# Retention followed by mixture of depths on one core: loads four ahead, a later fetch, q in 2 KB packets, a cap that also sums

## The chip, the core and the metric

The kernel runs on one core of a Trainium2 chip. The core has five engines with an instruction queue each: TensorE (PE in the profile; PEld are its weight loads), VectorE (DVE), ScalarE (ACT), GpSimd (POOL) and SyncE (SP), and 16 DMA engines that they share. The metric is the device time of one execution in microseconds; the median of three runs of the kernel before is 142.53 us (141.37 to 142.64).

## The reference

Two layers in a row. The first is a linear attention with decay, per batch (4), head (8) and token (768), with heads of 64. The second lets the 128 best-scored tokens of each batch through an expert with one hidden layer and leaves the others as they are.

```python
# q, k, v: [4, 8, 768, 64] float32
for t in range(S):
    state = gamma[None, :, None, None] * state + np.einsum('bhd,bhe->bhde', k[:, :, t], v[:, :, t])
    y[:, :, t] = scale * np.einsum('bhd,bhde->bhe', q[:, :, t], state)
...
x = y.transpose(0, 2, 1, 3).reshape(B, S, H * D)        # [4, 768, 512]
scores = np.einsum('bsd,d->bs', x, w_gate)
out = x.copy()
for b in range(B):
    top_idx = np.argpartition(-scores[b], capacity)[:capacity]      # capacity 128
    xe = x[b, top_idx]
    h = np.maximum(xe @ w1, 0.0)                                    # w1 [512, 1024]
    ye = h @ w2                                                     # w2 [1024, 512]
    g = 1.0 / (1.0 + np.exp(-scores[b, top_idx]))
    out[b, top_idx] = x[b, top_idx] + g[:, None] * ye
```

## The kernel before

The 768 tokens of a batch are three blocks of 256 (two chunks of 128 each); the four batches make 12 blocks, m = 0 to 11. The text calls the body of the main loop for block m "turn m".

**Loads and stores, on SP's queue.** `load(m)` (L54 to L63) brings q, k and v of a block, 512 KB each, into SBUF in float32. A partition holds two neighbouring tokens of all eight heads, so a contiguous piece is 512 bytes (two tokens of 64 floats). There are five buffers for each, and turn m begins with `load(m + 5)`. `put(m, xo)` (L246) stores the block's 256 output rows in two DMAs of 256 KB, one for the even and one for the odd tokens. SP works through its queue in order: block m's store stands behind load m + 5.

**Casts, on GpSimd.** `cast(m)` (L147) makes bfloat16 copies: q times a table of decays `gq`, k as it is, v times a table `gv`. Turn m casts block m + 2. GpSimd's queue also has the four DMAs of the expert's weights (w1s, w2s, in turns 1 to 4), the fetch of a batch's chosen rows, a product for the gate and the scatter of the result (`route_put`).

**A turn, on TensorE, VectorE and ScalarE.** In this order: the q transposes of block m + 1 (`transposes`, L159: eight on TensorE into PSUM, then one copy by ScalarE, L170); the second half of the block's own scores (`scores`, L173: 16 matmuls, then VectorE's multiply with the causal mask, L185); the state of the first chunk (`update`, L212); the k transposes of block m + 1; the outputs (`inside`, `across`, L191 to L210); `finish` (L232: ScalarE copies the output to SBUF, VectorE forms the token scores, `junk`, L242); the second chunk's state; `put`; the first half of the scores of block m + 1. Even and odd tokens of a chunk are kept as two halves, so the tokens of a row of scores stand as (even, odd), and the mask, the token numbers and the store are laid out for it.

**Routing and expert.** A batch's routing is written into slots of later turns by hand (`at(turn, place, ...)`, L404 to L419, run by `slot_work`). Place -1 is at the start of the turn before the casts, 0 to 4 lie between the steps above. In the turn after each block, `route_spread` (L259) turns a block's scores into a row and `route_beats` (L273) counts with VectorE which tokens beat which. After the batch's last block `route_beats` also caps the counts at 128 (`wonb`, L290, 128x5 elements), `route_ranks` (L295) adds up ranks on TensorE and `route_index` (L312) turns them into the 128 row numbers. One turn after that, `route_fetch` (L323) gathers the 128 rows from the output in HBM. It reads what `put` wrote, so it waits until the stores of the batch have landed; it is an instruction of GpSimd's queue and stands ahead of that turn's cast. Two turns later come `route_gate` and `route_turn` (the rows are transposed), then the expert: `ffn_up` twice, `ffn_down`, and in the next turn `ffn_add` (L386, VectorE), and then `route_put`, the scatter. The slots of turns 12 and later are worked off one after the other behind the loop.

The slots of a batch whose last block is m (L408 to L419) are, with turns counted from m: ranks and index at 1, fetch at 2, gate and turn at 4, expert at 5, add at 6, scatter at 7. The last blocks of the batches are 2, 5, 8 and 11.

Of the kernel before, what the change touches and what calls it, by code (L numbers as in the profile page):

```python
# [18 lines left out]
def kernel(ctx: ExitStack, tc: tile.TileContext, q, k, v, w_gate, w1, w2, capacity, out):  # L19
    nc = tc.nc  # L20
    B, H, S, D = q.shape
    C = 128
    NC = S // C
    T = 2 * C
    NM = S // T
    Dm = H * D
    F = w1.shape[1]
    cap = int(capacity)
# [22 lines left out]
    ctx.enter_context(tc.manual_schedule())  # L51


    raw = {}  # L54

    def load(m):
        b, r = divmod(m, NM)
        for nm, src in (("q", q), ("k", k), ("v", v)):
            t = loads.tile([128, H, 2, D], FT, name=nm + "f", tag=nm + "f")
            ap = src[b, :, r * T:(r + 1) * T, :]  # L60
            ap = bass.AP(tensor=ap.tensor, offset=ap.offset, ap=[[2 * D, 128], ap.ap[0], [1, 2 * D]])
            nc.sync.dma_start(t.rearrange("p h j d -> p h (j d)"), ap)
            raw[nm, m] = t  # L63

    load(0)
# [3 lines left out]

    pos_i = consts.tile([128, NM, 2], I32)
    nc.gpsimd.iota(pos_i, pattern=[[T, NM], [1, 2]], base=-MID, channel_multiplier=2)
    pos = consts.tile([128, 2 * NM], FT)
    nc.vector.tensor_copy(pos, pos_i.rearrange("p a b -> p (a b)"))
    lnsc = consts.tile([128, 1], FT)
    nc.vector.memset(lnsc, lnscale)
    gq = consts.tile([128, 2 * NM, H], FT)
    gv = consts.tile([128, 2 * NM, H], FT)
    for h in range(H):  # L80
        nc.scalar.activation(gq[:, :, h], pos, AF.Exp, bias=lnsc[:, 0:1], scale=lng[h])
    for h in range(H):
        nc.scalar.activation(gv[:, :, h], pos, AF.Exp, scale=-lng[h])
    ident = consts.tile([128, 128], BF)
# [2 lines left out]
    make_identity(nc, identf)  # L87

    causal = consts.tile([128, 2, 2, 64], BF)
    nc.gpsimd.memset(causal, 1.0)
    for u in range(2):
        rows = slice(u * 64, u * 64 + 64)
        nc.gpsimd.affine_select(out=causal[rows], in_=causal[rows], pattern=[[-1, 2], [1, 2], [2, 64]],
                                compare_op=OP.is_ge, fill=0.0, base=0, channel_multiplier=-2)

    ones = consts.tile([128, 128], BF)
# [5 lines left out]

    load(2)
    load(3)
    load(4)
    before = consts.tile([128, C], FT)
    tokrow = consts.tile([128, S], FT)
    slotcol = consts.tile([128, 1], FT)  # L110
# [1 line left out]
    def route_tables():  # L112
        nc.gpsimd.memset(before, TINY)
        nc.gpsimd.affine_select(out=before, in_=before, pattern=[[1, C]], compare_op=OP.is_gt,
                                fill=-TINY, base=0, channel_multiplier=-1)
        slot_i = consts.tile([128, 1], I32)
        nc.gpsimd.iota(slot_i, pattern=[[0, 1]], base=0, channel_multiplier=1)
        tok_i = loads.tile([128, S], I32, name="toki", tag="toki", bufs=1)
        nc.gpsimd.iota(tok_i.rearrange("p (c j t) -> p c j t", j=2, t=64), pattern=[[C, NC], [1, 2], [2, 64]],
                       base=0, channel_multiplier=0)  # L120
        nc.gpsimd.tensor_copy(slotcol, slot_i)
        nc.gpsimd.tensor_copy(tokrow, tok_i)
# [24 lines left out]
    def cast(m):  # L147
        r = m % NM
        kb = nats.tile([128, 2, H, D], BF, name="kb", tag="kb")
        vb = nats.tile([128, 2, H, D], BF, name="vb", tag="vb")  # L150
        qb = nats.tile([128, 2, H, D], BF, name="qb", tag="qb")
        nc.gpsimd.tensor_mul(qb, raw["q", m].rearrange("p h j d -> p j h d"),  # L152
                             gq[:, 2 * r:2 * r + 2, :, None].to_broadcast([128, 2, H, D]))
        nc.gpsimd.tensor_copy(kb, raw["k", m].rearrange("p h j d -> p j h d"))  # L154
        nc.gpsimd.tensor_mul(vb, raw["v", m].rearrange("p h j d -> p j h d"),  # L155
                             gv[:, 2 * r:2 * r + 2, :, None].to_broadcast([128, 2, H, D]))
        nat[m] = (kb, vb, qb)

    def transposes(m, nm):  # L159
        src = nat[m][2 if nm == "q" else 0]  # L160
        if nm == "q":
            pt = psT.tile([128, HP, 2, 2, 64], BF, name="pt", tag="pt")
        else:
            pt = psT.tile([128, 2, HP, 128], BF, name="pt", tag="pt")
        for j in range(2):
            for dd in range(HP):
                o = pt[:, dd, :, j, :] if nm == "q" else pt[:, j, dd, :]
                nc.tensor.transpose(o, src[:, j, 2 * dd:2 * dd + 2, :], ident)  # L168
        t = work.tile(list(pt.shape), BF, name=nm + "T", tag=nm + "T")
        nc.scalar.activation(t, pt, AF.Copy)  # L170
        tr[nm, m] = t

    def scores(m, part):  # L173
        qT, kT = tr["q", m], tr["k", m]
        pa = psA.tile([128, 2, 2, 2, C], FT, name="pa", tag="pa")
        for d in range(2):
            dd = 2 * part + d
            for j in range(2):
                for u in range(2):
                    for half in range(2):  # L180
                        r = slice(half * 64, half * 64 + 64)
                        nc.tensor.matmul(pa[u * 64:u * 64 + 64, half, d, j, :], kT[r, j, dd, u * 64:u * 64 + 64],  # L182
                                         qT[r, dd, u].rearrange("p j t -> p (j t)"), start=True, stop=True)
        am = work.tile([128, 2, 2, 2, C], BF, name="am", tag=f"am{part}")
        nc.vector.tensor_mul(am.rearrange("p a b c d -> p (a b) (c d)"), pa.rearrange("p a b c d -> p (a b) (c d)"),  # L185
                             causal.rearrange("p a b c -> p (a b c)")[:, None, :].to_broadcast([128, 4, 2 * C]))
        att[m, part] = am


# [13 lines left out]
    def across(m, u, py):  # L203
        i = 2 * m + u
        if i % NC == 0:
            return
        qT = tr["q", m]
        for dd in range(HP):
            nc.tensor.matmul(py[u][:, 2 * dd:2 * dd + 2, :], qT[:, dd, u].rearrange("p j t -> p (j t)"),  # L209
                             S_sb[i % 2][:, dd, :], start=False, stop=True, skip_group_check=True)  # L210

    def update(m, u):  # L212
# [32 lines left out]

    def put(m, xo):  # L246
        b, r = divmod(m, NM)
        for j in range(2):
            ap = out[b, r * T:(r + 1) * T, :]
            ap = bass.AP(tensor=ap.tensor, offset=ap.offset + j * Dm, ap=[[2 * Dm, 64], [C * Dm, 2], [1, Dm]])  # L250
            nc.sync.dma_start(ap, xo[j * 64:(j + 1) * 64])


    flat = out.rearrange("b s d -> (b s) d")
# [18 lines left out]
    def route_beats(b, r):  # L273
        st = batch[b]
        row, g, pr, won = st["row"], st["beats"], st["pr"], st["won"]
        if r:
            for u in range(2):
                c = 2 * r + u
                nc.vector.tensor_scalar(g[:, c, :r * T], row[:, :r * T], st["sc"][:, c:c + 1], float(c * C),
                                        OP.is_lt, OP.subtract, accum_out=won[:, c:c + 1])  # L280
        for u in range(2):
            c = 2 * r + u
            nc.vector.scalar_tensor_tensor(g[:, c, c * C:(c + 1) * C], pr[:, u, :], st["sc"][:, c:c + 1], before,
                                           OP.subtract, OP.is_lt)
        c = 2 * r + 1
        nc.vector.tensor_scalar(g[:, c, r * T:c * C], pr[:, 0, :], st["sc"][:, c:c + 1],
                                won[:, c:c + 1] if r else float(C), OP.is_lt, OP.subtract, accum_out=won[:, c:c + 1])
        if r == NM - 1:
            wonb = perb.tile([128, NC], BF, name="wonb", tag="wonb")
            nc.vector.tensor_scalar_min(wonb[:, 1:], won[:, 1:], float(cap))  # L290
            st["wonb"] = wonb


# [107 lines left out]
    def at(t, place, f, *args):  # L401
        slots.setdefault((t, place), []).append((f, args))

    for m in range(NBLK):  # L404
        b, r = divmod(m, NM)
        at(m + 1, 0, route_spread, b, r)
        at(m + 1, 1, route_beats, b, r)
        if r == NM - 1:  # L408
            at(m + 1, 3, route_ranks, b)
            at(m + 1, 4, route_index, b)  # L410
            at(m + 2, -1, route_fetch, b)
            at(m + 4, -1, route_gate, b)
            at(m + 4, 2, route_turn, b)
            at(m + 4, 4, route_sigmoid, b)
            at(m + 5, 0, ffn_up, b, 0)
            at(m + 5, 2, ffn_up, b, 1)
            at(m + 5, 3, ffn_down, b)
            at(m + 6, 1, ffn_add, b)
            at(m + 7, -1, route_put, b)  # L419

    def slot_work(t, place):
        for f, args in slots.pop((t, place), ()):
# [73 lines left out]
```

## Time and profile before

| | us |
|---|---|
| median of three runs | 142.53 |
| the profiled execution | 140.93 |
| its span, first to last instruction | 139.2 |
| TensorE busy (59% of the span) | 82.3 |
| VectorE busy (56%) | 77.7 |
| GpSimd busy (55%) | 76.7 |
| ScalarE busy (49%) | 67.6 |

No engine is busy for more than 59% of the span, and TensorE's mean granted clock is 0.843. DMA: SP's queue moved 25.43 MB in 41,040 packets, GpSimd's 4.20 MB in 2,240. From issue to landing a load takes 7.3 to 7.7 us, a store 5.3, a gather 4.6 (medians).

A line of a group or of a timeline names the line of the program, the engine, the operation and its tiles as output<-input. In the timeline the first number is the start in us and the second the duration; a bracket gives the idle time before it and what ended that. In the list of waits the three numbers are the us in total, the number of times and the longest. A row of windows has the stretch, its length, the busy time of PE, PEld, DVE, ACT and POOL with the number of instructions, the granted clock, the share of the DMA engines (it can exceed 1, as transfers overlap) and GB/s.

### The profile page before, as it was taken

To read this page: it belongs to the slowest core of one execution; us is meant where nothing else is said; L and a number is where in the kernel's file an instruction comes from. 1 tells how busy PE (TensorE), PEld (TensorE's weight loads), DVE (VectorE), ACT (ScalarE), POOL (GpSimd) and SP (SyncE) were. 2 spreads that over 40 slices of the span, in tenths; PEclk is the share of its full clock that TensorE was granted. 3 is DMA by queue.
4 is the path that set the end of the run, shared out by engine and by line. 5 is a ranking of instruction groups with operands and counts; after the bars stand their busy time and mean duration, and the time that the engine had idled before them with its cause. 6 is when DMAs were issued, how large, how long until landed. Compare 5 with 4: busy or idle time off the path is not lost. (4 is left out here: it accounts for less than half of the span.)

```text
span 139.2 us, 3845 instructions
## 1 busy us (share of the span) xinstructions
PE 82.3 (59%) x1612; PEld 63.6 (46%) x1612; DVE 77.7 (56%) x195; ACT 67.6 (49%) x135; POOL 76.7 (55%) x69
## 2 busy tenths in 40 slices
PE   0055939676984000009869389865948993686750
PEld 0044828555773000008767286555728852463610
DVE  2003366798998100004789787498977659942220
ACT  7233838876586000006663687565476744502310
POOL 6588999899662000089999109999902005103211
PEclk9999995998699855555677999997796899689996
DMA  3999999999999999999999989905314251512101
GB/s 79 306 290 301 301 290 291 292 291 240 305 284 316 224 353 300 311 297 348 295 250 325 315 237 321 329 19 111 119 39 111 80 147 48 133 57 75 75 0 75
DMA packets 43297, 29.86 MB, mean 215 GB/s; under 512 B 1168, under 2 KB 39056, under 8 KB 43280
## 3 DMA queue, kind: packets, MB, share of 16 engines
q1 hardware_dynamic: 41040, 25.43, 68.0%
q0 software_dynamic: 2240, 4.20, 13.2%
q8 instruction: 12, 0.20, 0.6%
q14 instruction: 5, 0.04, 0.1%
HBM read 24.38 MB, written 7.34 MB: 228 GB/s over the span
## 5 line engine op out<-in xcount | busy, mean ns | idle before, releaser
L185 DVE TENSOR_TENSOR am<-pa,causal 128x1024 bf16<-128x1024 f32 x24 | 29.3, 1220 | 37.5 <-PE pa L182 37.5
L168 PE MATMUL pt<-ident,qb 128*128 128x128 bf16 x96 | 8.9, 247 | 30.0 <-POOL qb L152 30.0
L170 ACT ACTIVATE qT<-pt 128x1024 bf16<-128x1024 bf16 x12 | 12.3, 1022 | 29.0 <-PE pt L168 28.6
L155 POOL TENSOR_TENSOR vb<-vf,gv 128x1024 bf16<-128x1024 f32 x12 | 22.8, 1899 | 3.1 <-DMA vf<-in_v_dram 3.0
L326 POOL DMA_INDIRECT xg<-out_dram,idx x4 | 4.4, 1090 | 36.1 <-DMA out_dram<-xo 16.9
L152 POOL TENSOR_TENSOR qb<-qf,gq 128x1024 bf16<-128x1024 f32 x12 | 22.9, 1905 | 2.0 <-DMA qf<-in_q_dram 1.9
L239 ACT ACTIVATE xo<-py 128x512 f32<-128x512 f32 x24 | 14.2, 598 | 15.0 <-DVE junk L242 12.5
L168 PEld LDWEIGHTS <-qb 128*128 128x128 bf16 x96 | 6.7, 110 | 31.2 <-POOL qb L152 30.7
L242 DVE SCALAR_TENSOR_TENSOR junk<-py,wgB 128x512 bf16<-128x512 f32 x24 | 15.7, 685 | 5.2 <-PE py L209 5.0
L230 ACT ACTIVATE S<-pst 64x256 bf16<-64x256 f32 x40 | 15.0, 374 | 5.6 <-PE pst L225 5.1
L182 PE MATMUL pa<-qT,kT 64*64 64x128 bf16 x384 | 11.8, 242 | 8.1 <-DVE am L185 6.3
L170 ACT ACTIVATE kT<-pt 128x1024 bf16<-128x1024 bf16 x12 | 12.3, 1022 | 3.6 <-PE pt L168 3.6
L154 POOL CAST kb<-kf 128x1024 bf16<-128x1024 f32 x12 | 12.4, 1036 | 1.2 <-DMA kf<-in_k_dram 1.2
L182 PEld LDWEIGHTS <-kT 64*64 64x64 bf16 x384 | 7.9, 118 | 11.1 <-issue 7.8
L394 POOL DMA_INDIRECT out_dram<-ye,idx x4 | 4.1, 1024 | 15.9 <-DVE ye L389 12.5
L168 PE MATMUL pt<-ident,kb 128*128 128x128 bf16 x96 | 10.6, 277 | 1.4 <-ACT qT L170 1.3
L199 PE MATMUL py<-vb,am 64*128 64x64 bf16 x384 | 10.5, 214 | 0.9 <-DVE am L185 0.9
L225 PE MATMUL pst<-vb,kb 64*64 64x64 bf16 x320 | 10.2, 208 | 0.1
L375 PE MATMUL ph<-xT,w1s 128*128 128x128 bf16 x128 | 8.9, 229 | 2.1 <-DVE junki L317 1.4
L168 PEld LDWEIGHTS <-kb 128*128 128x128 bf16 x96 | 9.1, 126 | 2.1 <-issue 1.4
L199 PEld LDWEIGHTS <-am 64*128 64x128 bf16 x384 | 8.6, 110 | 3.2 <-issue 1.5
L304 PE MATMUL pk<-beats,ones 128*128 128x512 bf16 (+3 forms) x32 | 6.9, 346 | 4.9 <-ACT xT L338 4.9
(63 smaller groups left out, 132.4 us busy)
## 6 DMA issues: line engine op xcount, KB each, us to landing
qf<-in_q_dram SPq DMA_DIRECT2D x12, 512.0 KB, 7.3
kf<-in_k_dram SPq DMA_DIRECT2D x12, 512.0 KB, 7.7
vf<-in_v_dram SPq DMA_DIRECT2D x12, 512.0 KB, 7.4
out_dram<-xo SPq DMA_DIRECT2D x24, 256.0 KB, 5.3
w1s<-in_moe_w_dram POOLq DMA_DIRECT2D x2, 512.0 KB, 8.2
w2s<-in_moe_w_dram POOLq DMA_DIRECT2D x2, 512.0 KB, 9.0
wgB<-in_moe_w_gate_dram SPq DMA_DIRECT2D x1, 256.0 KB
xg<-out_dram,idx POOLq DMA_INDIRECT x4, 4.6
```

The source lines that it names most:

```text
L152: nc.gpsimd.tensor_mul(qb, raw["q", m].rearrange("p h j d -> p j h d"), gq[:, 2 * r:2 * r + 2, :, None].to_broadcast([128, 2, H, D]))
L154: nc.gpsimd.tensor_copy(kb, raw["k", m].rearrange("p h j d -> p j h d"))
L155: nc.gpsimd.tensor_mul(vb, raw["v", m].rearrange("p h j d -> p j h d"), gv[:, 2 * r:2 * r + 2, :, None].to_broadcast([128, 2, H, D]))
L168: nc.tensor.transpose(o, src[:, j, 2 * dd:2 * dd + 2, :], ident)
L170: nc.scalar.activation(t, pt, AF.Copy)
L182: nc.tensor.matmul(pa[u * 64:u * 64 + 64, half, d, j, :], kT[r, j, dd, u * 64:u * 64 + 64], qT[r, dd, u].rearrange("p j t -> p (j t)"), st ...
L185: nc.vector.tensor_mul(am.rearrange("p a b c d -> p (a b) (c d)"), pa.rearrange("p a b c d -> p (a b) (c d)"), causal.rearrange("p a b c - ...
L199: nc.tensor.matmul(py[u][:, h, :], att[m, dd // 2][r, half, dd % 2, j, :], vb[r, j, h, :], start=(h == 0 and j == 0), stop=True, skip_grou ...
L225: nc.tensor.matmul(pstate[b][half * 64:half * 64 + 64, dd, :], kb[r, j, h, :], vb[r, j, h, :], start=(c == 0 and dd == 0 and j == 0), stop ...
L230: nc.scalar.activation(t[r, :, half * 64:half * 64 + 64], pstate[b][r], AF.Copy)
L239: nc.scalar.activation(xo[:, u, :], py[u].opt(), AF.Copy)
L242: nc.vector.scalar_tensor_tensor(junk, py[w].opt(), 1.0, wgB, OP.mult, OP.mult, accum_out=batch[b]["sc"][:, 2 * r + w:2 * r + w + 1])
```

## The change

Five edits in one:

- Turn m begins with `load(m + 4)` instead of `load(m + 5)`; there are still five buffers. Every store moves ahead of one load on SP's queue.
- For batches 0 and 1 the fetch and all that follows it are one turn later (fetch at 3 turns behind the last block, expert at 6, scatter at 8). Batches 2 and 3 keep their turns.
- q is loaded in two DMAs of 256 KB, one for the even and one for the odd heads: a partition holds eight neighbouring tokens of one head of each, in pieces of 2 KB; the partitions go over 32 groups of eight tokens (outermost) and four heads. The table `gq` follows this layout and is made by two ScalarE instructions from per-partition scales, which VectorE works out ahead. The q transposes (eight, as before) leave the token groups apart in PSUM, and ScalarE's copy to `qT` puts them in order.
- With the tokens in order, the mask, the token numbers and the store lose the (even, odd) layout; the two stores of a block are now one per chunk.
- The cap `wonb` becomes an instruction that also accumulates a sum (`s1`), which nothing reads.

```diff
+            if nm == "q":
+                t = loads.tile([128, 2, 8, D], FT, name="qf", tag="qf")
+                for half in range(2):
+                    nc.sync.dma_start(t[:, half].rearrange("p j d -> p (j d)"),
+                                      bass.AP(tensor=ap.tensor, offset=ap.offset + half * S * D,
+                                              ap=[[8 * D, T // 8], [2 * S * D, HP], [1, 8 * D]]))
...
-    for h in range(H):
-        nc.scalar.activation(gq[:, :, h], pos, AF.Exp, bias=lnsc[:, 0:1], scale=lng[h])
+    for half in range(2):
+        nc.scalar.activation(gq[:, :, :, half].rearrange("p a b -> p (a b)"), posp, AF.Exp,
+                             bias=lnsc[:, 0:1], scale=lngc[:, half:half + 1])
...
-    load(4)
...
         nc.gpsimd.tensor_mul(qb, raw["q", m].rearrange("p h j d -> p j h d"),
-                             gq[:, 2 * r:2 * r + 2, :, None].to_broadcast([128, 2, H, D]))
+                             gq[:, r, :, :, None].to_broadcast([128, 8, 2, D]))
...
         if nm == "q":
-            pt = psT.tile([128, HP, 2, 2, 64], BF, name="pt", tag="pt")
+            pt = psT.tile([128, 8, T // 8, HP], BF, name="pt", tag="pt")
+            for i in range(8):
+                nc.tensor.transpose(pt[:, i].rearrange("p s g -> p (s g)"), src[:, i], ident)
+            t = work.tile([128, HP, T], BF, name="qT", tag="qT")
+            nc.scalar.activation(t.rearrange("p g (s i) -> p g s i", i=8), pt.rearrange("p i s g -> p g s i"), AF.Copy)
...
-        for j in range(2):
-            ap = out[b, r * T:(r + 1) * T, :]
-            ap = bass.AP(tensor=ap.tensor, offset=ap.offset + j * Dm, ap=[[2 * Dm, 64], [C * Dm, 2], [1, Dm]])
-            nc.sync.dma_start(ap, xo[j * 64:(j + 1) * 64])
+        for u in range(2):
+            nc.sync.dma_start(out[b, r * T + u * C:r * T + (u + 1) * C, :], xo[:, u, :])
...
-            nc.vector.tensor_scalar_min(wonb[:, 1:], won[:, 1:], float(cap))
+            s1 = perb.tile([128, 1], FT, name="s1", tag="s1")
+            nc.vector.tensor_scalar(wonb[:, 1:], won[:, 1:], float(cap), 0.0, OP.min, OP.add, accum_out=s1)
...
-            at(m + 2, -1, route_fetch, b)
-            at(m + 4, -1, route_gate, b)
-            at(m + 4, 2, route_turn, b)
-            at(m + 4, 4, route_sigmoid, b)
-            at(m + 5, 0, ffn_up, b, 0)
-            at(m + 5, 2, ffn_up, b, 1)
-            at(m + 5, 3, ffn_down, b)
-            at(m + 6, 1, ffn_add, b)
-            at(m + 7, -1, route_put, b)
+            d = m + 3 if b < B - 2 else m + 2
+            at(d, -1, route_fetch, b)
+            at(d + 2, -1, route_gate, b)
+            at(d + 2, 2, route_turn, b)
+            at(d + 2, 4, route_sigmoid, b)
+            at(d + 3, 0, ffn_up, b, 0)
+            at(d + 3, 2, ffn_up, b, 1)
+            at(d + 3, 3, ffn_down, b)
+            at(d + 4, 1, ffn_add, b)
+            at(d + 5, -1, route_put, b)
...
-        if m + 5 < NBLK:
-            load(m + 5)
+        if m + 4 < NBLK:
+            load(m + 4)
```

More of the change, by code (lines that the diff above doesn't have):

```diff
@@ L58, in load @@
         for nm, src in (("q", q), ("k", k), ("v", v)):
-            t = loads.tile([128, H, 2, D], FT, name=nm + "f", tag=nm + "f")
             ap = src[b, :, r * T:(r + 1) * T, :]
-            ap = bass.AP(tensor=ap.tensor, offset=ap.offset, ap=[[2 * D, 128], ap.ap[0], [1, 2 * D]])
-            nc.sync.dma_start(t.rearrange("p h j d -> p h (j d)"), ap)
+            if nm == "q":
[4 more added lines that the diff above has]
+                                              ap=[[8 * D, T // 8], [2 * S * D, HP], [1, 8 * D]]))
+            else:
+                t = loads.tile([128, H, 2, D], FT, name=nm + "f", tag=nm + "f")
+                ap = bass.AP(tensor=ap.tensor, offset=ap.offset, ap=[[2 * D, 128], ap.ap[0], [1, 2 * D]])
+                nc.sync.dma_start(t.rearrange("p h j d -> p h (j d)"), ap)
             raw[nm, m] = t
@@ L68 @@
     nc.sync.dma_start(wgB, bass.AP(tensor=w_gate.tensor, offset=w_gate.offset, ap=[[0, 128], [1, Dm]]))
+    part_i = consts.tile([128, 3], I32)
+    nc.gpsimd.iota(part_i[:, 0:1], pattern=[[0, 1]], base=0, channel_multiplier=1)
+    free_i = consts.tile([128, NM, 8], I32)
+    nc.gpsimd.iota(free_i, pattern=[[T, NM], [1, 8]], base=-MID, channel_multiplier=0)
+    grp_i = consts.tile([128, HP], I32)
+    nc.gpsimd.iota(grp_i, pattern=[[1, HP]], base=0, channel_multiplier=0)
     pos_i = consts.tile([128, NM, 2], I32)
@@ L73 @@
     nc.gpsimd.iota(pos_i, pattern=[[T, NM], [1, 2]], base=-MID, channel_multiplier=2)
+    lnsc = consts.tile([128, 1], FT)
+    nc.vector.memset(lnsc, lnscale)
+    lngt = consts.tile([128, 2, HP], FT)
+    for h in range(H):
+        nc.vector.memset(lngt[:, h % 2, h // 2:h // 2 + 1], lng[h])
+    nc.vector.tensor_scalar(part_i[:, 1:2], part_i[:, 0:1], 2, 3, OP.arith_shift_right, OP.logical_shift_left)
+    nc.vector.tensor_single_scalar(part_i[:, 2:3], part_i[:, 0:1], HP - 1, OP.bitwise_and)
@@ new lines @@
+    part = consts.tile([128, 3], FT)
+    nc.vector.tensor_copy(part, part_i)
+    grp = consts.tile([128, HP], FT)
+    nc.vector.tensor_copy(grp, grp_i)
+    posq = consts.tile([128, 8 * NM], FT)
+    nc.vector.tensor_copy(posq, free_i.rearrange("p a b -> p (a b)"))
+    lngc = consts.tile([128, 2], FT)
+    for half in range(2):
+        one4 = consts.tile([128, HP], FT, name=f"one4{half}")
+        nc.vector.scalar_tensor_tensor(one4, grp, part[:, 2:3], lngt[:, half, :], OP.is_equal, OP.mult,
+                                       accum_out=lngc[:, half:half + 1])
@@ L74 @@
+    posp = consts.tile([128, 8 * NM], FT)
+    nc.vector.tensor_scalar_add(posp, posq, part[:, 1:2])
+    gq = consts.tile([128, NM, 8, 2], FT)
+    gv = consts.tile([128, 2 * NM, H], FT)
+    for half in range(2):
+        nc.scalar.activation(gq[:, :, :, half].rearrange("p a b -> p (a b)"), posp, AF.Exp,
+                             bias=lnsc[:, 0:1], scale=lngc[:, half:half + 1])
     pos = consts.tile([128, 2 * NM], FT)
     nc.vector.tensor_copy(pos, pos_i.rearrange("p a b -> p (a b)"))
-    lnsc = consts.tile([128, 1], FT)
@@ L77 @@
-    nc.vector.memset(lnsc, lnscale)
-    gq = consts.tile([128, 2 * NM, H], FT)
-    gv = consts.tile([128, 2 * NM, H], FT)
-    for h in range(H):
-        nc.scalar.activation(gq[:, :, h], pos, AF.Exp, bias=lnsc[:, 0:1], scale=lng[h])
     for h in range(H):
@@ L87 @@
     make_identity(nc, identf)
-    causal = consts.tile([128, 2, 2, 64], BF)
+    causal = consts.tile([128, 2, C], BF)
     nc.gpsimd.memset(causal, 1.0)
@@ L94 @@
         rows = slice(u * 64, u * 64 + 64)
-        nc.gpsimd.affine_select(out=causal[rows], in_=causal[rows], pattern=[[-1, 2], [1, 2], [2, 64]],
+        nc.gpsimd.affine_select(out=causal[rows], in_=causal[rows], pattern=[[-1, 2], [1, C]],
                                 compare_op=OP.is_ge, fill=0.0, base=0, channel_multiplier=-2)
@@ L118, in route_tables @@
         tok_i = loads.tile([128, S], I32, name="toki", tag="toki", bufs=1)
-        nc.gpsimd.iota(tok_i.rearrange("p (c j t) -> p c j t", j=2, t=64), pattern=[[C, NC], [1, 2], [2, 64]],
+        nc.gpsimd.iota(tok_i, pattern=[[1, S]],
                        base=0, channel_multiplier=0)
@@ L150, in cast @@
         vb = nats.tile([128, 2, H, D], BF, name="vb", tag="vb")
-        qb = nats.tile([128, 2, H, D], BF, name="qb", tag="qb")
+        qb = nats.tile([128, 8, 2, D], BF, name="qb", tag="qb")
         nc.gpsimd.tensor_mul(qb, raw["q", m].rearrange("p h j d -> p j h d"),
-                             gq[:, 2 * r:2 * r + 2, :, None].to_broadcast([128, 2, H, D]))
+                             gq[:, r, :, :, None].to_broadcast([128, 8, 2, D]))
         nc.gpsimd.tensor_copy(kb, raw["k", m].rearrange("p h j d -> p j h d"))
@@ L161, in transposes @@
         if nm == "q":
-            pt = psT.tile([128, HP, 2, 2, 64], BF, name="pt", tag="pt")
+            pt = psT.tile([128, 8, T // 8, HP], BF, name="pt", tag="pt")
[3 more added lines that the diff above has]
+            nc.scalar.activation(t.rearrange("p g (s i) -> p g s i", i=8), pt.rearrange("p i s g -> p g s i"), AF.Copy)
         else:
             pt = psT.tile([128, 2, HP, 128], BF, name="pt", tag="pt")
-        for j in range(2):
[L166 to L170, printed above, removed]
+            for j in range(2):
+                for dd in range(HP):
+                    nc.tensor.transpose(pt[:, j, dd, :], src[:, j, 2 * dd:2 * dd + 2, :], ident)
+            t = work.tile([128, 2, HP, 128], BF, name="kT", tag="kT")
+            nc.scalar.activation(t, pt, AF.Copy)
         tr[nm, m] = t
@@ L182, in scores @@
                         nc.tensor.matmul(pa[u * 64:u * 64 + 64, half, d, j, :], kT[r, j, dd, u * 64:u * 64 + 64],
-                                         qT[r, dd, u].rearrange("p j t -> p (j t)"), start=True, stop=True)
+                                         qT[r, dd, u * C:(u + 1) * C], start=True, stop=True)
         am = work.tile([128, 2, 2, 2, C], BF, name="am", tag=f"am{part}")
         nc.vector.tensor_mul(am.rearrange("p a b c d -> p (a b) (c d)"), pa.rearrange("p a b c d -> p (a b) (c d)"),
-                             causal.rearrange("p a b c -> p (a b c)")[:, None, :].to_broadcast([128, 4, 2 * C]))
+                             causal.rearrange("p a b -> p (a b)")[:, None, :].to_broadcast([128, 4, 2 * C]))
         att[m, part] = am
@@ L208, in across @@
         for dd in range(HP):
-            nc.tensor.matmul(py[u][:, 2 * dd:2 * dd + 2, :], qT[:, dd, u].rearrange("p j t -> p (j t)"),
+            nc.tensor.matmul(py[u][:, 2 * dd:2 * dd + 2, :], qT[:, dd, u * C:(u + 1) * C],
                              S_sb[i % 2][:, dd, :], start=False, stop=True, skip_group_check=True)
@@ L247, in put @@
         b, r = divmod(m, NM)
-        for j in range(2):
-            ap = out[b, r * T:(r + 1) * T, :]
-            ap = bass.AP(tensor=ap.tensor, offset=ap.offset + j * Dm, ap=[[2 * Dm, 64], [C * Dm, 2], [1, Dm]])
-            nc.sync.dma_start(ap, xo[j * 64:(j + 1) * 64])
+        for u in range(2):
+            nc.sync.dma_start(out[b, r * T + u * C:r * T + (u + 1) * C, :], xo[:, u, :])
     flat = out.rearrange("b s d -> (b s) d")
```

## The prediction

> **What bounds the kernel now.** I read the 40 slices first, then the list of waits, then GpSimd's and the transfers' timelines, and last windows of a few microseconds. The slices (each 3.48 us):
>
> ```profile
> PE   0055939676984000009869389865948993686750
> DVE  2003366798998100004789787498977659942220
> POOL 6588999899662000089999109999902005103211
> DMA  3999999999999999999999989905314251512101
> GB/s 79 306 290 301 301 290 291 292 291 240 305 284 316 224 353 300 311 297 348 295 250 325 315 237 321 329 19 111 119 39 111 80 147 48 133 57 75 75 0 75
> ```
>
> Three stretches are to be seen. The transfers are full until about 90 us. Inside that, from 45 to 62, every engine stands still. After 90 the transfers are nearly idle and the engines work off the last blocks to 139. The waits say who holds the hole:
>
> ```profile
> DVE am L185 <- PE pa L182: 37.5, 12, 18.6
> PE pt L168 <- POOL qb L152: 30.0, 5, 19.2
> POOL xg L326 <- DMA out_dram<-xo: 16.9, 1, 16.9
> ```
>
> VectorE waits for TensorE, TensorE for GpSimd's cast of q, and GpSimd for a store: the fetch of batch 0's rows stands ahead of cast(6) in GpSimd's queue and waits until block 2's store has landed. GpSimd's timeline, then SP's store:
>
> ```profile
> 41.93 0.77 POOL L136 DMA_DIRECT2D w2s<-in_moe_w_dram  x1
> 59.63 1.12 POOL L326 DMA_INDIRECT xg<-out_dram,idx  x1 [16.92 <-DMA out_dram<-xo]
> 60.77 1.91 POOL L152 TENSOR_TENSOR qb<-qf,gq 128x1024 bf16<-128x1024 f32 x1
> ...
> 83.39 1.10 POOL L326 DMA_INDIRECT xg<-out_dram,idx  x1 [6.42 <-DMA qf<-in_q_dram]
> ...
> 99.31 1.89 POOL L155 TENSOR_TENSOR vb<-vf,gv 128x1024 bf16<-128x1024 f32 x1
> ```
>
> ```profile
> 52.43 2.21 SPq L251 DMA_DIRECT2D out_dram<-xo  x2
> ```
>
> Block 2 was computed by 32 us, but on SP its store stands behind loads 6 and 7 and was issued at 52.4. The same happens, smaller, to batch 1 (6.4 us). So the hole does not starve the transfers; it costs because the casts, done at 101.2, end some 12 us after the last load (about 89, since the windows of one microsecond show full transfers to 90 with block 6's store at the end). From there each turn (loop body m; it starts with the q transposes of block m+1) is bound by its own chain: turns 8 to 10 start at 88.5, 92.5 and 104.1, turn 11's scores run at 113.8, its score sums end at 118.98, and 20.2 us of one batch's routing and expert follow to 139.2.
>
> **Part 1, the order (loads four ahead, fetch of batches 0 and 1 a turn later).** SP: five loads instead of six stand ahead of block 0's store, and so on. A load is 1.57 MB and a store 0.52; at 298 GB/s (the mean of the full slices) 5.3 and 1.76 us. Load m then has one more store ahead of it: +1.76 us for the last one. Block 2's store comes one load earlier: from a landing near 59.6 to about 54. GpSimd meets the fetch after cast(6), whose v I put at 50 (v of block 5 landed at 40.1; then a store, a load and a share of the weights), so at 52 to 53: a wait of 1 to 2 us in place of 16.9. If the store landed as late as now, the wait would be 6.6 us, and three casts of 4.85 us against 7 us of transfers per block would win it back: 1 us at most. Fetch 1 waits for block 5's store, right behind load 9: about 2 us.
>
> The price: batch 0's expert moves from turn 7 to 8, batch 1's from 10 to 11. Turn 7 with it took 8.6 us and turn 4 without one 4.8, turn 10 with it 9.7: so an expert is worth 4 to 4.9 us in either place, and moving it inside the loop costs nothing. But batch 1's second half now stands in turn 11 ahead of the last score row: TensorE stood idle 2.56 us before that row (waiting for the score sums), and 16 matmuls of up (1.07) and 8 of down (2.08) with the relu between go there, about 3.7. VectorE then has the expert's add (0.75) ahead of the last beats. Together 1.95 us more in the tail. GpSimd's queue has put(1) ahead of the last fetch: 1.0 us, and landed some 4.4 us after the add, before the last index is ready. On SP the store of block m, which waits for ScalarE's copies, now has load m+5 behind it. Between v of block m+1, which starts turn m, and the end of load m+4 lie three loads and stores, 21 us; less the 7.4 us from issue to landing, 13 us are left for the cast and a turn of 5 to 9: no load is late.
>
> **Part 2, q in packets of 2 KB.** 9,216 packets fewer, 12 DMAs more on SP's queue: the first issues, into an empty queue, took 0.43 and 0.57 us, the later ones 1.74 because the transfers were full, so the issues are covered; uncovered they would be 12 x 0.5 = 6 us. What it does for the rate:
>
> ```profile
> 3.00:8.00 5.00, 0.84 (x8) 0.77 (x8) 0.00 (x0) 1.51 (x12) 3.10 (x3) 1.00 1.19 306
> ...
> 46.00:48.00 2.00, 0.00 (x0) 0.00 (x0) 0.00 (x0) 0.00 (x0) 0.00 (x0) 0.94 1.19 226
> ...
> 50.00:52.00 2.00, 0.00 (x0) 0.00 (x0) 0.00 (x0) 0.00 (x0) 0.00 (x0) 0.50 1.10 362
> ```
>
> (the last number of a row is GB/s). Loads in 512 B packets alone run at 291 to 306; where rows of stores and weights mix in, it goes from 226 to 362. 6.29 MB of q take 21.1 us at 298, 17.4 at 362 and 27.8 at 226: from 3.7 us won to 6.7 lost. I take 2 won, since windows at 344 to 362 (four of them) are commoner than the low ones. The Trainium skill (DMA: Bandwidth & Descriptors, Specifications) speaks against it: it gives 512 B as the least transfer for line rate, by which packets of 2 KB win nothing; the last load would then land 2 us later, which the sum has room for except 1 us. With 2 us won and 1.76 given, the last load lands at about 89 as now.
>
> The evacuation of qT (L170, 1.02 us, 12 times) now reads its eight token groups interleaved, bf16 elements 256 bytes apart. No row reads like that. Nearest: kT, the same size read in order, 1.02 us; and xT, half as many elements but four bytes each, 0.60, so not bytes but elements are paid. I take 1.02 and keep 2.04 as the upper end; a gain is excluded, as nothing gets smaller. The Trainium skill (SBUF — State Buffer, Door 1: The DMA port swizzle) says that PSUM has lines of 8 bytes and that non-contiguous access slows matmuls down; were it so for ScalarE's reads, the sum would be rival 2's; no row here shows it. The q transposes keep their number and size (247 ns), GpSimd's q multiply its 1.90 us (vb, whose form stays, takes as much).
>
> Preamble: 11 more VectorE instructions (rows of 0.06 to 0.17 us, 2 us in all from 1.1) and 3 iotas; ScalarE's gq shrinks from 8 to 2 and would be ready near 4.2, ahead of q's landing at 5.2. Uncovered it would cost up to 1 us, at a start that the transfers lead anyway.
>
> **Part 3, the cap with a sum.**
>
> ```profile
> 74.61 2.38 DVE L290 TENSOR_SCALAR wonb<-won 128x5 bf16<-128x5 f32 x1
> ...
> 99.45 1.79 DVE L290 TENSOR_SCALAR wonb<-won 128x5 bf16<-128x5 f32 x1
> ```
>
> The two others take 0.17. The slow two end where a GpSimd multiply ends (75.08+1.89 and 99.31+1.89); the fast two ran beside an idle GpSimd. The accumulating forms on this engine (L279, 16 times from SBUF) keep 468 to 746 ns for their two or three sizes with GpSimd busy, so I take 0.3 us: 2.1 and 1.5 us won in turns 6 and 9, where the score sums, ScalarE's copy and the second ranks stand behind.
>
> **The sum.** Transfers pace the casts: v of block 11 at 89, 10 at 81.5, 9 at 74.5, 8 at 67.5. q of block 9 is cast at 72.6 (after vb(8) and the gate product, 1.27): turn 8 starts there, not at 88.5. It takes 4.06 (as now) + 4.9 (expert) = 9: turn 9 starts at 81.6 (its q is ready at 80.3). Turn 9 now takes 11.5; batch 0's like, turn 3, with ranks but with neither the turn of xg nor the slow cap, took 7.4; with the add 0.75: 8.1, to 89.7. Turn 10 as turn 4 (4.8) and the turn of xg with its copies (2): to 96.5; k of block 11 is cast by 88, so nothing waits. Turn 11: 5.2 to the score sums plus 1.3 for the first half of up: 103.0, against 118.98. Tail 20.2 + 1.95 = 22.2: span 125.2. The profiled execution took 140.93 us with a span of 139.2: 1.73 around it, so 126.9; the median shown is 1.1% above that execution: 128.3.
>
> **The rivals.**
> 1. The turns do not get shorter: the transfers stay full in both, turns 9 to 11 keep their 26.5 us from 81.6, and the hole is paid in small waits. 108.1 + 22.2 + 1.73 = 132.0, on the median 133.5. For it: turn 10 and 11 keep all their work. Against: the 2.0 us wait for xT and 1.6 of the cap are named in the trace.
> 2. qT's copy takes twice as long. Three turns that bound the path (8, 9, 10): +3.1 us, 131.4; three times as long, 134.5.
> 3. Slower: the new q pattern (32 rows of 2 KB outermost, heads inside) runs the q loads at under half the rate. 6.29 MB at 150 GB/s take 42 us, 23 more than taken; 21 of them reach the path: 149. It decides once q's rate is below about 175 GB/s (36 us). The lowest window of the trace, 226, gives 8.7 more than taken, about 135. Speaks against: all 16 engines stay in use for other 2 KB rows (stores) without such a fall.
> 4. The fetch still waits as long, because block 2's store does not come earlier: the wait moves behind cast(6); 1 us at most, 129.5.
>
> **Numbers.** Forecast 0.55; rival 1 0.22; 2 0.12; 3 0.04; 4 0.03; 0.04 for a mishap that ends between 136 and 144. About 1% (1.4 us) is what a measurement of this kernel can tell from no change. Low end: 362 GB/s for q, 1.7 us more won, and turns 9 to 11 two microseconds shorter still, with a clock that no longer falls to 0.5 after the hole: 124. High end: rival 1 and 226 GB/s halfway, 136. Faster 0.94, same 0.02, slower 0.04.
>
> **What would show it.** The fetch's wait of 16.9 is below 4 us and turn 5 starts near 47 instead of 62.7; cast(11) ends near 91 instead of 101.2; the four caps take 0.3 each; qT's copy is at 1.02; the last score sums end near 103 and 22 us follow. I am wrong if the transfers are full until 95, if ScalarE's qT rows are at 2 us, or if turns 9 to 11 still take 26 us.

## The result, and the profile after

| | before | after |
|---|---|---|
| median of four runs each, side by side | 142.58 us (141.37 to 146.64) | 127.16 us (126.48 to 129.42) |
| ratio, 95% interval | | 0.8928 [0.8844, 0.9012] |
| profiled execution, its span | 140.93, 139.2 | 127.14, 125.4 |
| TensorE, VectorE, GpSimd busy | 82.3, 77.7, 76.7 | 81.3, 75.1, 77.3 |
| packets of SP's queue | 41,040 | 32,016 |

Ratios, here and below, compare only runs in which neither kernel was in its slower state, so they can differ a little from the quotient of the medians. The time is 1.1 us below the number forecast. Hardly any work has gone; idle time has. The slices after, each 3.14 us:

```profile
PE   0053775958499729349939499995438697785820
POOL 6649999999853798480699969848940300330330
PEclk9999997799859995865799859999965579999995
DMA  2999999999999999999999999999406104203202
GB/s 63 282 335 304 344 304 324 310 309 317 246 310 257 368 295 255 337 244 325 363 336 314 334 351 332 299 315 391 170 25 200 56 5 167 84 0 84 84 0 84
```

The hole, a run of zeros in every engine's row, is gone, and GpSimd is done with the casts at nearly the moment the transfers are (88 us, where the DMA row falls from 9 to 4). Something else is new just there: TensorE's row goes 5, 4, 3 and its granted clock 6, 5, 5, 7, where the last turns should run quickly. The list of waits names both:

```profile
DVE am L220 <- PE pa L217: 23.6, 12, 8.8
PE pt L196 <- POOL qb L184: 20.7, 7, 6.7
POOL xg L360 <- DMA qf<-in_q_dram: 2.4, 2, 1.4
DVE idx L354 <- DMA out_dram<-ye,idx: 3.4, 1, 3.4
```

The gather's wait for a store, 16.9 us, is no longer in the list; two waits of 1.4 and 1.0 us are left, put down to the landing of q. The last row has no counterpart before: VectorE, on its way to write the row numbers `idx` of batch 2, waits for the scatter of batch 0. GpSimd's timeline shows the first gather, the end of the last cast, that scatter and the next gather:

```profile
51.84 1.12 POOL L360 DMA_INDIRECT xg<-out_dram,idx  x1 [1.42 <-DMA qf<-in_q_dram]
...
86.75 1.90 POOL L187 TENSOR_TENSOR vb<-vf,gv 128x1024 bf16<-128x1024 f32 x1 [0.46 <-DMA vf<-in_v_dram]
88.81 1.08 POOL L428 DMA_INDIRECT out_dram<-ye,idx  x1 [0.16 <-issue]
...
92.82 1.08 POOL L360 DMA_INDIRECT xg<-out_dram,idx  x1 [1.63 <-DVE idx L354]
```

and VectorE's timeline what stands behind:

```profile
88.24 0.09 DVE L351 DVE_READ_ACCUMULATOR junki<-pk,slotcol,tokrow 128x1 f32 x1
91.73 0.21 DVE L354 TENSOR_SCALAR idx<-acc 128x1 int32<-128x1 f32 x1 [3.41 <-DMA out_dram<-ye,idx]
91.86 1.22 DVE L220 TENSOR_TENSOR am<-pa,causal 128x1024 bf16<-128x1024 f32 x1
```

and TensorE's what waits for that:

```profile
88.78 0.41 PE L234 MATMUL py<-vb,am 64*128 64x64 bf16 x16
93.13 0.61 PE L234 MATMUL py<-vb,am 64*128 64x64 bf16 x16 [3.94 <-DVE am L220]
```

The same 16 matmuls take 0.41 us before the wait and 0.61 after it. Windows of 2 us (columns as before: the third number from the end is the granted clock) say why:

```profile
90.00:92.00 2.00, 0.00 (x0) 0.00 (x0) 0.27 (x2) 0.17 (x1) 1.19 (x1) 0.96 0.34 131
92.00:94.00 2.00, 0.87 (x20) 0.78 (x21) 1.86 (x5) 0.00 (x0) 1.08 (x1) 0.50 0.01 4
...
100.00:102.00 2.00, 2.00 (x35) 1.67 (x34) 0.93 (x5) 0.94 (x3) 0.00 (x0) 0.50 0.00 0
```

One idle stretch of 4 us on TensorE comes with 10 us at half clock (92 to 102), and those are the turns that set the end.

Why there is such a wait: `idx` comes from a pool with two buffers per tile, so batch 2's `idx` is written where batch 0's stood, and batch 0's scatter still reads that. `idx` of batch 2 is written in turn 9. Before, batch 0's scatter was issued in turn 9 too, ahead of cast(11); the change moves it to turn 10, behind cast(11) in GpSimd's queue. So the row numbers of batch 2, and with them the mask multiply of block 10, stand behind the last cast, and so behind the last load.

### The profile page after: what moved, and what is told of

Same layout as the page of the kernel before. It is cut to its first block, busy times and chain, and to the rows that moved or that the text cites. A ratio compares the mean times of both kernels' runs of the same rounds, so it can differ in the third digit from the quotient of the medians.

```text
span 125.4 us, 3891 instructions
## 1 busy us (share of the span) xinstructions
PE 81.3 (65%) x1605; PEld 64.0 (51%) x1612; DVE 75.1 (60%) x217; ACT 66.3 (53%) x129; POOL 77.3 (62%) x72
## 3 DMA queue, kind: packets, MB, share of 16 engines
q1 hardware_dynamic: 32016, 25.43, 66.8%
## 5 line engine op out<-in xcount | busy, mean ns | idle before, releaser
L198 ACT ACTIVATE qT<-pt 128x1024 bf16<-128x1024 bf16 x12 | 12.3, 1023 | 20.6 <-PE pt L196 20.6
L196 PEld LDWEIGHTS <-qb 128*128 128x128 bf16 x96 | 7.0, 114 | 22.2 <-POOL qb L184 21.7
L217 PE MATMUL pa<-qT,kT 64*64 64x128 bf16 x384 | 12.5, 253 | 7.3 <-DVE am L220 5.9
L205 ACT ACTIVATE kT<-pt 128x1024 bf16<-128x1024 bf16 x12 | 12.3, 1022 | 2.9 <-PE pt L203 2.8
L217 PEld LDWEIGHTS <-kT 64*64 64x64 bf16 x384 | 8.5, 124 | 10.0 <-issue 6.9
L234 PE MATMUL py<-vb,am 64*128 64x64 bf16 x384 | 10.0, 209 | 4.4 <-DVE am L220 4.4
L234 PEld LDWEIGHTS <-am 64*128 64x128 bf16 x384 | 8.1, 107 | 6.7 <-DVE am L220 4.7
L203 PE MATMUL pt<-ident,kb 128*128 128x128 bf16 x96 | 9.9, 264 | 1.5 <-ACT qT L198 1.4
L409 PE MATMUL ph<-xT,w1s 128*128 128x128 bf16 x128 | 9.8, 242 | 1.3 <-ACT xT L372 0.7
L203 PEld LDWEIGHTS <-kb 128*128 128x128 bf16 x96 | 8.6, 120 | 2.6 <-POOL kb L186 1.2
L409 PEld LDWEIGHTS <-w1s 128*128 128x128 bf16 x128 | 8.9, 110 | 1.7 <-issue 1.6
L260 PEld LDWEIGHTS <-kb 64*64 64x64 bf16 x320 | 8.8, 127 | 1.1 <-issue 0.6
```

Of the source, the lines that this page charges most:

```text
L196: nc.tensor.transpose(pt[:, i].rearrange("p s g -> p (s g)"), src[:, i], ident)
L203: nc.tensor.transpose(pt[:, j, dd, :], src[:, j, 2 * dd:2 * dd + 2, :], ident)
L234: nc.tensor.matmul(py[u][:, h, :], att[m, dd // 2][r, half, dd % 2, j, :], vb[r, j, h, :], start=(h == 0 and j == 0), stop=True, skip_grou ...
L260: nc.tensor.matmul(pstate[b][half * 64:half * 64 + 64, dd, :], kb[r, j, h, :], vb[r, j, h, :], start=(c == 0 and dd == 0 and j == 0), stop ...
L409: nc.tensor.matmul(ph[:, j, :], w1s[:, dd, ff * 128:(ff + 1) * 128], st["xT"][:, dd, :], start=(j == 0 and dd == 0), stop=True, skip_group ...
```

## The experiments

Every experiment had runs of the kernel before beside it, with medians between 141.46 and 141.83 us. Executions of one kernel lie up to 6.2 us apart here, so medians are given with lowest and highest, and the ratio to before with its interval where there is one. The kernel after, timed again beside some of the experiments, had a median of 128.25 us (125.99 to 130.32), so a difference from 127.16 below is about 1 us uncertain.

**The parts of the change, one at a time.** First the order alone: the kernel before with loads four ahead and the late gather, q and cap as they were.

```diff
+            d = m + 3 if b < B - 2 else m + 2
+            at(d, -1, route_fetch, b)
...
-        if m + 5 < NBLK:
-            load(m + 5)
+        if m + 4 < NBLK:
+            load(m + 4)
```

> The kernel before with loads four ahead and the fetch of batches 0 and 1 a turn later, q and cap as they were. Theory (the recorded one: the order fills the hole): fetch 0 waits under 4 us instead of 16.9 and turn 5 starts near 47; against the changed kernel (127.2) it lacks the cap (1.5 us in turn 9, the 2.1 of turn 6 hidden by transfers) and q's faster packets (about 2 us of transfers): 129.5 to 132. Rival (the transfers are the bound, and the order alone only spreads the hole): above 136.

134.84 us (132.65 to 135.7): missed by 3 to 5. The gather's wait is down to 2.75 us, so the mechanism is there, but `idx` waits 5.58 us and the last cast ends at 95.24 instead of 88.65. Then the order and the new cap, with the old q (shown as a difference from the kernel after):

```diff
-            if nm == "q":
-                t = loads.tile([128, 2, 8, D], FT, name="qf", tag="qf")
...
+            t = loads.tile([128, H, 2, D], FT, name=nm + "f", tag=nm + "f")
...
-        for u in range(2):
-            nc.sync.dma_start(out[b, r * T + u * C:r * T + (u + 1) * C, :], xo[:, u, :])
+        for j in range(2):
...
```

> The changed kernel with q loaded in 512-byte pieces as before, tokens as (even, odd), stores as before (order and cap changed only). Theory: q's packets bring 2 us of transfer time, of which about 1 reaches the end: casts of block 11 end 2 us later (near 91), 128 to 129. Rival 1 (512 bytes are already at line rate): 127.2, casts at 89. Rival 2 (the transfers pace every turn to the end): 2 to 3.5 us more, 129.5 to 131.

134.57 us (134.09 to 136.14), ratio 0.9585 [0.9523, 0.9648]: both numbers missed. q in 2 KB packets, with tokens in order, is worth 134.57 - 127.16 = 7.4 us (6.3 against the repeat), not 1 to 2. The last cast and the row numbers in this kernel's timelines of GpSimd

```profile
92.14 1.90 POOL L154 TENSOR_TENSOR vb<-vf,gv 128x1024 bf16<-128x1024 f32 x1 [0.33 <-DMA vf<-in_v_dram]
```

and of VectorE

```profile
94.06 0.08 DVE L317 DVE_READ_ACCUMULATOR junki<-pk,slotcol,tokrow 128x1 f32 x1
97.11 0.21 DVE L320 TENSOR_SCALAR idx<-acc 128x1 int32<-128x1 f32 x1 [2.96 <-DMA out_dram<-ye,idx]
```

stand 5.4 us later than after the change (92.14 against 86.75, 97.11 against 91.73): the row numbers move exactly with the last cast. The cap alone, put back into the changed kernel:

```diff
-            nc.vector.tensor_scalar(wonb[:, 1:], won[:, 1:], float(cap), 0.0, OP.min, OP.add, accum_out=s1)
+            nc.vector.tensor_scalar_min(wonb[:, 1:], won[:, 1:], float(cap))
```

> The changed kernel with the cap as it was. Theory: VectorE's cap is held while a GpSimd multiply runs; in turn 6 the cover is the transfers, in turn 9 it is on the path: one or two caps of 1.5 to 2.4 us in the trace, 128.5 to 129.5. Rival 1: both count: 130.8. Rival 2: the wait for the row-number buffer in turn 10 (3.4 us) swallows it: 127.2.

128.28 us (125.64 to 131.12), not to be told from 127.16 or 128.25, so it does not decide between the first theory and rival 2. Two of the four caps are held again, as VectorE's timeline shows; both end where a GpSimd multiply ends (62.43 + 1.90 and 85.17 + 1.90):

```profile
62.87 1.48 DVE L323 TENSOR_SCALAR wonb<-won 128x5 bf16<-128x5 f32 x1
...
86.31 0.79 DVE L323 TENSOR_SCALAR wonb<-won 128x5 bf16<-128x5 f32 x1
```

And the new cap alone in the kernel before:

```diff
+            s1 = perb.tile([128, 1], FT, name="s1", tag="s1")
+            nc.vector.tensor_scalar(wonb[:, 1:], won[:, 1:], float(cap), 0.0, OP.min, OP.add, accum_out=s1)
```

> The kernel before with the summing cap alone. Recorded theory: both held caps of the trace before (2.38 and 1.79 us) lie in turns that VectorE's chain bounds (6 and 9): up to 3.6 us, 137.5 to 139.5 beside 141.5. Rival (the cap is held only if a GpSimd multiply happens to run, as it was in no turn of the run with the order alone; and what follows waits for something else): 140 to 142.

138.91 us (137.41 to 139.53), ratio 0.9907 [0.9763, 1.0051]: the four caps take 0.16 us each, the median is inside the range expected, and the interval holds no change as well. The size stays open between a loss of 0.7 and a gain of 3.4 us, which is wider than the 1% that the prediction reckoned a measurement could tell. In the order-only kernel the old cap took 0.17 to 0.20 every time; there the new one is worth 134.84 - 134.57 = 0.3 us, which is less than the spread.

**The wait for the row numbers.** A third buffer for `idx`, and nothing else, in the changed kernel:

```diff
-        idx = perb.tile([128, 1], I32, name="idx", tag="idx")
+        idx = perb.tile([128, 1], I32, name="idx", tag="idx", bufs=3)
```

> The changed kernel with three buffers instead of two for the row numbers (idx). Theory: VectorE's wait of 3.4 us before idx of batch 2 (it waits until batch 0's scatter, which reads the same buffer and is now a turn later, has landed) is on the path, and TensorE runs at a clock of 0.5 to 0.6 after it: without it the last score sums end 3.4 to 5.5 us earlier, 122 to 124. Rival: turn 10 is then held by the casts of block 11 (vb ends at 88.7) or by the gather of batch 2: under 1.5 us won, 125.7 to 127.

122.63 us (121.0 to 123.82), as expected, and the fastest of all the kernels here: every run of it is below every run of the kernel after. VectorE's timeline of it:

```profile
89.01 0.08 DVE L351 DVE_READ_ACCUMULATOR junki<-pk,slotcol,tokrow 128x1 f32 x1
89.13 0.21 DVE L354 TENSOR_SCALAR idx<-acc 128x1 int32<-128x1 f32 x1
89.26 1.21 DVE L220 TENSOR_TENSOR am<-pa,causal 128x1024 bf16<-128x1024 f32 x1
```

No bracket stands behind `idx`, the granted clock is 1.00 from 88 to 100 us, and turn 10 takes 7.6 us (q transposes at 86.52, turn 11's scores at 94.12) instead of 12.8. The last score sums end at 99.36 instead of 104.27, although the last cast ends 1.2 us later (89.84): the wait and the clock behind it cost 4.9 us in this pair of traces and 4.5 in the medians (5.6 against the repeat). The same buffer in the kernel with the order and the cap but the old q:

> Order and cap changed, q as before, three idx buffers (134.6 with two). Theory: the wait for batch 0's scatter is what ties the end to the last cast (put(0) stands behind it on GpSimd), so with it gone the slower transfers reach the end only through the cast of k of block 11: 125.5 to 128, that is 3 to 5 us behind the 122.6 of the new q, not 7.4. Rival (the transfers pace everything to the end): 129.5 to 131, the same 7.4 behind.

127.95 us (127.4 to 128.84), ratio 0.9087 [0.8987, 0.9186]. Against the old q with two buffers the third one is worth 134.57 - 127.95 = 6.6 us, so order and cap bring 13.9 us (141.83 - 127.95) without the new q, as soon as the row numbers no longer stand behind the last cast. Against 122.63 with the new q, the new q is worth 5.3 us here: slightly over the 3 to 5 expected, and not the rival's 7.4. The theory's picture is only partly right, though: the last casts of the two kernels lie 5.2 us apart (they end at 95.07 and 89.84) and the last score sums 5.1 (104.45 and 99.36), so the slower transfers still reach the end in full. TensorE waits 1.28 us for the cast of q ahead of turn 10 (91.25).

**The rate of the loads by itself.** A kernel that only loads, on SP's queue: all of q in 512 B pieces, k in 2 KB pieces, v in 512 B, q again in 2 KB, each tile looked at by one small VectorE copy. Attention, routing and expert are left out.

```diff
+    for src, f, nm in ((q, load_512, "qa"), (k, load_2k, "kb"), (v, load_512, "va"), (q, load_2k, "qb")):
+        for m in range(NBLK):
+            t = f(m, src, nm)
+            nc.vector.tensor_copy(seen[:, n, :], t[:, 0:1024:512])
```

> Only loads, 12 blocks each: q in 512-byte pieces, k in 2 KB pieces (the new q pattern), v in 512-byte pieces, q in 2 KB pieces; a copy of two elements of each block and one small store; attention, routing and expert are left out. Theory (the packets carry the gain): 295 to 302 GB/s in the stretches of 512 bytes, 360 to 390 in those of 2 KB (from 298 to 321 with a third of the loads changed: 380). Rival (512 bytes are at line rate, the gain came from the order of the stores): the same rate in all four.

One execution. Windows inside the four stages (with stretch, length, busy time of VectorE and GpSimd, clock, DMA share, GB/s):

```profile
10.00:20.00 10.00, 1.01 (x6) 0.00 (x0) 1.00 1.20 290
24.00:32.00 8.00, 1.01 (x6) 0.00 (x0) 1.00 1.06 384
...
44.00:52.00 8.00, 0.77 (x5) 0.00 (x0) 1.00 1.20 290
...
64.00:70.00 6.00, 0.74 (x5) 0.00 (x0) 1.00 1.06 387
```

290 GB/s for 512 B and 384 to 387 for 2 KB, both times, whichever tensor it is. The 6.29 MB of q take 21.7 us at 290 and 16.3 at 386: 5.4 us, the distance by which the last cast moved between the old q and the new. Whether it is the length of a piece or the order in which the new pattern walks through memory was not tried apart.

**The order edit, half by half.** First the gathers back to two turns behind the last block, in the changed kernel:

```diff
-            d = m + 3 if b < B - 2 else m + 2
+            d = m + 2
```

> The changed kernel with the fetch of batches 0 and 1 back at two turns behind the last block. Recorded theory (the later fetch is what fills the hole): GpSimd waits from 44 to about 52 for block 2's store, some 7.5 us, and again about 6 us for block 5's: 130 to 133. New theory (the later fetch costs as much as it brings: it makes the index of batch 2 wait for batch 0's scatter, 3.4 us and a slow clock behind it, and lengthens the tail by 1 to 2): casts of block 11 end 4 us later, near 93, but no wait of VectorE before idx, and a tail of 20.2 us: 124 to 127.5.

130.2 us (129.0 to 130.81), ratio 0.9208 [0.91, 0.9315]: the recorded theory met, the new one missed. GpSimd's timeline:

```profile
54.77 1.12 POOL L360 DMA_INDIRECT xg<-out_dram,idx  x1 [7.86 <-issue]
...
78.00 1.12 POOL L360 DMA_INDIRECT xg<-out_dram,idx  x1 [5.87 <-PE ph L409]
```

(The releasers named had long been done; what the gather reads is the store.) With loads four ahead (and the new q and cap) the waits of 16.9 and 6.4 become 7.9 and 5.9, the last cast ends at 95.85, and there is no wait for the row numbers, as batch 0's scatter is back in its old turn. Then the other half, loads five ahead with the late gather:

```diff
-        if m + 4 < NBLK:
-            load(m + 4)
+        if m + 5 < NBLK:
+            load(m + 5)
```

> The changed kernel with loads five ahead again. Theory: block 2's store lands one load later, near 57, and block 5's near 82; the fetches then hold GpSimd 6 us each; the first is won back, the second is not, and the casts of block 11 end near 92: 130 to 132. Rival (with the later fetch the place of the stores no longer matters): 126.5 to 128.

130.73 us (128.85 to 131.69), ratio 0.9286 [0.9191, 0.938], as expected: waits of 7.08 and 4.22; the last cast ends at 90.39 (92 expected), and `idx` still waits 1.85 us. Each half alone gets rid of a little over half of the first wait. Last, with the third buffer, only batch 0 late:

```diff
-            d = m + 3 if b < B - 2 else m + 2
+            d = m + 3 if b == 0 else m + 2
```

> The changed kernel with three idx buffers, and only batch 0's fetch later (batch 1's expert back in turn 10). Theory: batch 1's fetch in turn 7 holds GpSimd some 6 us for block 5's store, ahead of cast(9), and turns 8 to 11 start later; the tail is 1 to 2 us shorter: 125 to 130, slower than the 122.6 of three buffers alone. Rival (the casts win it back and the shorter tail remains): 120.5 to 122.

133.38 us (132.8 to 135.91), ratio 0.9435 [0.9315, 0.9554]: slower than with both late, as expected, but by 10.8 us instead of 2 to 7. GpSimd's timeline shows the hole where it went:

```profile
75.80 1.10 POOL L360 DMA_INDIRECT xg<-out_dram,idx  x1 [5.83 <-DMA qf<-in_q_dram]
```

TensorE stands still for 9.40 us ahead of turn 8's q transposes, and turns 8 to 10 behind it take 9.4, 8.1 and 9.7 us. Why that costs so much is seen beside the kernel with both gathers early, whose second gather waited as long (it has two buffers for `idx`, and no wait for them). Turn 8's start in this kernel's timeline of TensorE

```profile
78.89 1.03 PE L196 MATMUL pt<-ident,qb 128*128 128x128 bf16 x8 [9.40 <-POOL qb L184]
```

and in that one's

```profile
81.11 0.62 PE L196 MATMUL pt<-ident,qb 128*128 128x128 bf16 x8 [1.05 <-POOL qb L184]
```

That kernel starts turn 8 2.2 us later, but its last score sums end 3.0 us earlier (108.32 against 111.32). There batch 0's expert runs in turn 7, in the time in which TensorE waits here; here it runs in turn 8, behind the wait, and turn 8 takes 9.4 us instead of 4.7. Part of that is the clock, 0.50 from 80 to 84 us; the two were not told apart. So a step moved a turn later can land behind a hole that it used to fill.

**The expert's add in the tail.** Every batch's add one place later, which puts batch 1's behind the last beats, with three buffers:

```diff
-            at(d + 4, 1, ffn_add, b)
+            at(d + 4, 2, ffn_add, b)
```

> Three idx buffers, and the expert's add moved from ahead of the beats to behind them in the same turn. Recorded theory (the add with its wait for down stands ahead of batch 3's last beats and costs 1.95 us of tail): 120.7 to 121.7, the index of batch 3 comes 1 to 2 us earlier after the last score sums. Rival (what follows needs the add's PSUM buffer, so the wait only moves behind the beats to the transposes of batch 2's rows): 122 to 123.5, as with three buffers alone. In both the last score sums end near 99.

123.27 us (122.78 to 124.56), ratio 0.8837 [0.8736, 0.8939], against 122.63 (121.0 to 123.82): nothing won, as the rival expected. The beats do come sooner: the cap is done 3.0 us after the last score sums (99.81) instead of 4.8. But the row numbers follow after 6.7 us instead of 6.6, because the first ranks on TensorE start 3.7 us after the sums here and 3.8 without the edit. TensorE's timeline here

```profile
103.52 1.14 PE L338 MATMUL pk<-beats,ones 128*128 128x128 bf16 x6 [0.20 <-DVE ye L423]
```

and with three buffers alone

```profile
103.15 1.14 PE L338 MATMUL pk<-beats,ones 128*128 128x128 bf16 x6 [0.69 <-ACT xT L372]
```

Here the ranks wait for the add itself, so the wait has moved and not gone. That a PSUM buffer is the reason fits, but was not tried by itself.

## Why the prediction was right, and where not

**The hole, right.** The gather's waits are 1.4 and 1.0 us (below 4 forecast), turn 5 starts at 46.40 (near 47), and the casts follow the transfers. Both halves of the edit are needed, and the loads' half more than the working said, in which the casts win back a late store (rival 4, "1 us at most"). With loads five ahead the wait is 7.08 us (6.6 forecast), a second of 4.22 follows, and the time is 3.6 us longer (2.5 against the repeat).

**q in 2 KB packets, mis-sized.** The step "I take 2 won" was wrong, and so were its bounds for the pure load rate: 5.4 us of transfers are won, outside 3.7. The best mixed window, 362 GB/s, was taken for the upper end; 2 KB loads alone run at 386, and 512 B loads alone at 290 where 298 was taken. (The lowest full window that was read is 214, from 82 to 83 us, and not 226; nothing hangs on it. Of SP's packets 9,024 went, not 9,216.) The rule of the Trainium skill that was weighed against it (DMA: Bandwidth & Descriptors, Specifications: 512 B is the least transfer for line rate) is not borne out here: 290 against 386 GB/s, with piece length and order changed together. It would have made the step worth nothing. The step's other half, "+1.76 us for the last one", was too small: in the kernel with the old q the last load's multiply starts at 92.14, some 3 us behind the 89 read from the kernel before. In the sum the last cast ends at 88.65 where 91 was forecast.

**A wait that no step had.** The part on the order priced each moved instruction's time, but not what the moved scatter holds: the buffer of `idx`. "k of block 11 is cast by 88, so nothing waits" failed on VectorE, not on the casts. It costs 4.5 us (127.16 against 122.63), and 6.6 with the old q, which is why order and cap without the new q reached only 134.57. "Moving it inside the loop costs nothing", said of the expert, was likewise priced without its surroundings: the kernel with only batch 0 late shows a turn 8 of 9.4 us instead of 4.7 behind a wait.

**The turns, right only in sum.** Turn 8 took 8.45 us (9 forecast), turn 9 5.8 (8.1), turn 10 12.8 (6.8), turn 11 to its score sums 6.05 (6.5). Turns 9 and 10 together are 18.6 where 14.9 was forecast, 3.7 more, against TensorE's new wait of 3.94; with it gone turn 10 takes 7.6. Score sums end at 104.27, only 1.3 after the 103.0 forecast, because turns 8 to 10 began 1.4, 2.0 and 4.3 us earlier than forecast. By this turns 9 to 11, from 79.62, took 24.6 us, near the 26 that the prediction named as its refutation and rival 1 kept; it is the new wait that does it, for with the third buffer they take 19.0 (80.38 to 99.36), less than the 21.4 of the sum. The hit at 127.2 is therefore partly luck: the sum of a gain that was put too low and a loss that was not seen.

**The tail, smaller.** 21.1 us, not 22.2: the added 1.95 were 0.9. With batch 1's expert back in turn 10 the tail is 20.3 and 20.2 us (both gathers early; only batch 0 late), so the 0.9 comes with batch 1's expert, as the working said; moving VectorE's add alone does not remove them.

**The cap, right in the instruction, not in the gain.** It takes 0.16 us plus 0.08 for the read of the sum. The 2.1 and 1.5 us are not added to the rest: in the order-only kernel the old cap is never held, in the changed kernel it would be for 1.48 and 0.79. What decides is whether a GpSimd multiply happens to run, and the edit's own worth is below what these runs tell apart.

**qT's copy, right.** 1.02 us per copy (1,023 ns, twelve times), so rival 2 falls, and the q transposes take 255 ns against 247. Rival 1's turns came close (24.6 against 26.5), but its reason falls with the 19.0 us above, rival 3 with 386 GB/s, rival 4 with the gather's waits.

## What to carry to other kernels

When a step is moved to a later turn, its tiles are held a turn longer: for each of them look up who writes that buffer next, on which in-order queue that writer stands, and what stands behind it. A forecast that comes true is not yet a confirmed working; the turns' own times showed two errors that had cancelled, and the larger of them was worth a one-word edit and 4.5 us. And the rate of a load pattern is better measured by itself than read from windows in which stores and gathers are mixed in.

## What was not expected of the hardware

- Loads in pieces of 2 KB run at 384 to 387 GB/s, in pieces of 512 B at 290, with the DMA engines full in both (shares 1.06 and 1.20). The pieces also walk through memory in a different order.
- ScalarE reads bfloat16 elements 256 bytes apart in PSUM at the speed of neighbouring ones: 1,023 ns for 128x1024 against 1,022 for kT.
- With one idle stretch of 3.94 us TensorE's granted clock was 0.50 for 10 us, though it was busy for all of the windows 94 to 96 and 100 to 102. The Trainium skill (TensorE: Matmul & The Clock Gate, Part 1) puts the fall at an idle window of about 3.4 us, and the return after about 3.4 us of sustained work. Here the fall came some 2.7 us into the idle time (an estimate from the 0.96 in the window 90 to 92), and the half clock lasted longer, with a window of 0.89 busy us in 2 between.
- The clock can fall without such a stretch: with the add moved it was 0.69, 0.50 and 0.95 in the windows from 94 to 100, and TensorE's longest idle time in the five microseconds before was 1.33 us.
- A VectorE instruction on 5 elements per partition can take 0.17 or 1.48 us, depending on what GpSimd does at the time; the form that also accumulates took 0.16 in every trace that has it. In the kernel after, two of its four (at 60.26 and 84.72) ran while a GpSimd multiply did (from 59.81 and 83.41, 1.90 us each).
